# P.V in four groups of four and five steps instead of six groups of three, in the attention of an attention, top-1 MoE and soft MoE kernel on one core

## The chip, the cores and the metric

The kernel runs on one core of one Trainium2 chip. The metric is the device time of one execution in microseconds; lower is better. The engines are called PE (TensorE matmul), PEld (its weight loads), DVE (VectorE), ACT (ScalarE), POOL (GpSimd) and SP (SyncE, which issues DMAs).

## What is computed

Three layers follow each other. Inputs are q, k, v of 4 batches, 8 heads, 1152 positions, 64 wide; the change concerns the first layer alone.

```python
def _attn_ref(q, k, v):
    q_pool = q.reshape(B, H, S // 2, 2, D).mean(axis=3)
    scores = np.matmul(q_pool, k.transpose(0, 1, 3, 2)) / np.sqrt(D)
    scores = scores - np.max(scores, axis=-1, keepdims=True)
    attn = np.exp(scores)
    attn = attn / (np.sum(attn, axis=-1, keepdims=True) + 1e-09)
    return np.matmul(attn, v).astype(np.float32)
...
def reference(...):
    x = attention output, as (B * S / 2, H * D)
    x = _moe_ref(x, ...)    # top-1 of 8 experts: logits, softmax gate, relu FFN of the chosen expert
    return _moe2_ref(x, ...)    # soft MoE with 32 slots
```

## The kernel before

The attention works on 16 pairs of heads, p = 0 to 15 (4 batches of 4 pairs, HP = 4). A pair has 576 pooled queries in two halves u of 288 columns, and 1152 keys in 9 blocks c of 128 (NKB). A **unit** is one (u, c, j): half, key block and head j of the pair. A pair has 36 units, pos = 0 to 35, and a unit has two matmuls into one score buffer of three in PSUM: S1 (line 266, the high part of the product) and S2 (line 272, the low part, with the row maximum subtracted in the same matmul), and then an exponential on ACT (line 276). Two units, j = 0 and 1, make a **step**, 18 to a pair; a step's exponentials lie in one of nine buffers e (EB = 9).

P.V (lines 278 to 289) takes a step's exponentials and two blocks of V, two matmuls per step that the profile shows as four records. It is not done step by step but in **groups** (line 301): three steps at a time (GS = 3), at positions 8, 14, 20, 26, 32 and, for the last three steps of a pair, at position 2 of the next pair (LAG = 3). With each group the steps' exponentials are added up on POOL (accadd, lines 291 to 299), for the softmax sums; in the last pair DVE does most of that. A buffer e comes free when its P.V and its addition have been done.

Between the units, other work of the attention is placed by hand, in a table from position to calls (at, line 569; run at lines 682 and 683, after the unit's S2):

- maxpiece (line 204): a matmul for one of 27 pieces of the row maxima of a later pair, into a PSUM tile of the tag mx (three buffers, shared with nps, sg, sgT, tp and the routing's tiles), and a reduction on DVE (line 219). Positions: MA1, MA, MB, and for pair 0 P0 and P1.
- maxred and maxrow (MR): the maxima of the next pair are gathered on DVE, transposed on PE (nps, line 235) and written into the operand QL on DVE.
- prep (PREP, PREP0) prepares the operands of pair p + 2: two casts kc on ACT (KC), qadd (qs), one cast qc on ACT (QC), two subtractions kl on DVE (KL, line 189), and ql (QLc, line 198), with DMAs on SP that spread each to the tiles KS, KH, QS and QL. qadd and ql run on DVE, in some pairs on POOL.
- fin0, fin1, fin2 (FA for the first half of the queries, FE, FB or FZ for the second, FC): sums and routing logits (sg, lines 319 to 323, and a copy on ACT), their transposes (sgT) with small DVE steps, and the transposes of P.V (tp, line 346) with a product on DVE.
- route (line 352): when a batch's four pairs are done, the routing of its tokens, a queue of small DVE and PE steps, of which line 686 lets one go per permitted position; and 24 **hot** steps per batch, pairs of ACT operations (lines 387 and 388), given out ahead of each group by the table NHOT (line 41, or four a group in the last pairs). A table matmul (tbp) ends it.
- ahead.split: in pairs 14 and 15 a cast on ACT and a subtraction on DVE (lines 796 and 797) for the next layer's first weights, at positions 2, 8, 14, 20, 26 and 32.

The order on every engine is the order in which these calls are made; nothing is reordered. At one position the calls run in this order: S1, S2, the table's work, one constant, one routing step, the hot steps, the group.

Of the kernel before, what the change touches and what calls it, by code (L numbers as in the profile page):

```python
# [87 lines left out]
def attention(ctx, tc, g):  # L88
# [476 lines left out]

    for p in range(n + 1):
        work = {}

        def at(pos, *fs):
            work[pos] = work.get(pos, []) + list(fs)  # L570
# [3 lines left out]
        if p == 0:  # L574
            for i, m in enumerate(range(NP0, NP)):
                at(P0[0] + i * P0[1] // 8, mp(0, m))
            at(P0[0] + P0[1] + 1, lambda: maxred(0, [3, 4]))
# [8 lines left out]
        elif p + 1 < n:
            for pos, m in zip(MA1, range(24)) if p == 1 else zip(MA, range(3, 24)):
                at(pos, mp(p + 1, m))
            if p + 2 < n:
                for pos, m in zip(MB, (24, 25, 26, 0, 1, 2)):  # L590
                    at(pos, mp(p + 2, m))
        if p + 2 < n:
            for pos, f in zip(PREP0 if p == 0 else PREP, prep(p + 2, nc.gpsimd if p == 0 or p >= HP and p % HP < 2 else None)):
                at(pos, f)
        if p < n:
            if p + 1 < n:
                late = 1 if p == 0 else 0
                at(MR[0] + late, lambda: maxred(p + 1, [0, 1, 2, 3, 4]))
                at(MR[1] + late, lambda: maxrow(p + 1))
            late = 4 if p in (0, n - 1) else 2 if p >= HP and p % HP == 0 else 0  # L600
            at(FA[0] + late, lambda: fin0(p, 0))
            at(FA[1] + late, lambda: fin1(p, 0))
# [1225 lines left out]
```

## Time and profile before

| | us |
|---|---|
| runs: median (lowest to highest, 3 runs) | 801.65 (800.77 to 803.76) |
| profiled execution | 804.16 |
| its span, first to last instruction | 802.4 |
| attention, first S1 of pair 0 to last S2 of pair 15 (19.44 to 490.60 of the span) | 471.16 |
| PE busy, of the span | 781.1 |
| DVE, POOL and ACT busy, of the span | 557.7, 470.2 and 463.9 |
| mean granted TensorE clock | 0.998 |

Times are those of one profiled execution, by the hardware profiler. Matmuls are pipelined: their starts are recorded and their ends are modelled, so distances between starts say more than durations. Where a timeline has an idle time in brackets, it is the engine's ahead of that row, with the instruction that ended it. The granted clock is 1 at 2.4 GHz and 0.5 at 1.2 GHz.

### The profile page before, as it was taken

Reading aid. Unit: us, or ns where it says so; the run is one execution under the profiler, and the core shown is the slowest. Engines: PE = TensorE matmul, PEld = TensorE weight load, DVE = VectorE, ACT = ScalarE, POOL = GpSimd, SP = SyncE. Lnnn points to the kernel's source line nnn. Section 1 sums busy time; section 2 is a strip of 40 time slices with the busy share of each in tenths; the row PEclk is TensorE's granted clock in tenths of the full one; section 3 lists DMA queues with packets and bytes.
Section 4 is the critical chain, followed back from the end, with each engine's and each line's share of the span. In section 5 each row is a group of like instructions: output and inputs, shape, how many; then the busy total and the mean of one; then the engine's idle time right before and its main releaser. Section 6 shows DMA issues by size and latency. Waiting matters only on the chain.

```text
span 802.4 us, 16064 instructions
## 1 busy us (share of the span) xinstructions
PE 781.1 (97%) x5696; PEld 598.4 (75%) x5696; DVE 557.7 (70%) x1163; ACT 463.9 (58%) x1101; POOL 470.2 (59%) x429
## 2 busy tenths in 40 slices
PE   5899999999999999999999999999999999999997
PEld 5667777777777777777766667799898789988467
DVE  6867777778777878776878786766666566675242
ACT  5456665665776657776556964355554546554232
POOL 6968899999988987888988964310302211020200
PEclk9999999999999999999999999999999999999999
DMA  9796648675655675664564220677776788976997
GB/s 325 169 270 157 171 138 205 171 217 159 150 157 142 164 210 143 163 169 135 136 151 123 79 81 1 215 236 269 255 286 216 240 293 279 328 256 242 381 394 243
DMA packets 55625, 162.84 MB, mean 203 GB/s; under 512 B 12154, under 2 KB 19626, under 8 KB 51434
## 3 DMA queue, kind: packets, MB, share of 16 engines
q1 hardware_dynamic: 49668, 134.76, 56.0%
q10 hardware_dynamic: 2592, 17.43, 5.9%
q0 software_dynamic: 3280, 9.57, 3.8%
q8 instruction: 47, 0.77, 0.4%
q14 instruction: 38, 0.31, 0.1%
HBM read 110.45 MB, written 10.89 MB: 151 GB/s over the span
## 4 chain that ended last, share of the span: by engine, by line
PE 90%; DVE 6%; ACT 1%; DMA 1%; issue 1%; POOL 0%; ACTq 0%; DVEq 0%
PE pv L286 18%; PE sc L266 12%; PE sc L272 9%; PE mps L217 8%; PE hp L805 4%; PE hp L807 4%; PE hp L806 4%; PE yp L819 4%; PE yp L821 4%; PE yp L820 4%; DVE mxp L219 2%; PE sg L319 2%; PE op L1570 2%; PE hp L1553 2%; PE tp L346 2%; PE tp L784 1%
## 5 line engine op out<-in xcount | busy, mean ns | idle before, releaser
L299 POOL TENSOR_TENSOR acc<-acc,e 128x576 f32<-128x576 f32 x214 | 316.8, 1481 | 20.2 <-ACT e L276 6.7
L276 ACT ACTIVATE e<-sc 128x288 f32<-128x288 f32 x576 | 225.0, 411 | 132.6 <-PE sc L272 113.5
L219 DVE TENSOR_REDUCE mxp<-mps 128x1 f32<-128x384 f32 x432 | 220.5, 549 | 93.9 <-PE mps L217 87.0
L266 PE MATMUL sc<-QS,KS 128*128 128x288 f32 x576 | 185.4, 330 | 1.2 <-ACT e L276 1.0
L272 PE MATMUL sc<-QL,KH 69*128 69x288 f32 x576 | 169.6, 297 | 0.4 <-DVE QL L260 0.3
L286 PE MATMUL pv<-e,V 128*64 128x288 f32 x1152 | 162.1, 417 | 0.0
L266 PEld LDWEIGHTS sc<-QS,KS 128*128 128x128 f32 x576 | 108.8, 189 | 53.1 <-issue 21.2
L217 PE MATMUL mps<-KS,QS 128*128 128x384 f32 x384 | 135.5, 357 | 10.4 <-ACT QS L487 7.1
L286 PEld LDWEIGHTS pv<-e,V 128*64 128x64 f32 x1152 | 74.6, 137 | 61.3 <-issue 23.4
L272 PEld LDWEIGHTS sc<-QL,KH 69*128 69x128 f32 x576 | 108.8, 189 | 0.8 <-POOL QL L490 0.5
L797 DVE TENSOR_TENSOR wlo<-wraw,whi 128x512 fp32r<-128x512 f32 x136 | 90.2, 687 | 23.5 <-ACT whi L796 21.1
L796 ACT CAST whi<-wraw 128x512 fp32r<-128x512 f32 x136 | 79.2, 618 | 11.1 <-DMA wraw<-in_w 5.7
L217 PEld LDWEIGHTS mps<-KS,QS 128*128 128x128 f32 x384 | 74.3, 194 | 15.2 <-ACT QS L487 7.5
L805 PE MATMUL hp<-xh,whi 128*128 128x256 f32 x256 | 73.3, 286 | 0.0
L807 PE MATMUL hp<-xh,wlo 128*128 128x256 f32 x256 | 71.7, 280 | 0.0
L806 PE MATMUL hp<-xl,whi 128*128 128x256 f32 x256 | 71.5, 279 | 0.0
L962 POOL DMA_INDIRECT ls<-both,xidx x17 | 18.0, 1058 | 88.3 <-DVE both L944 45.3
L812 ACT ACTIVATE hh<-hp 128x256 fp32r<-128x256 f32 x64 | 24.6, 384 | 76.4 <-PE hp L807 72.1
L775 POOL DMA_INDIRECT xg<-xs,xidx x17 | 18.8, 1106 | 84.6 <-PE tp L784 51.5
L297 POOL TENSOR_TENSOR acc<-e 128x576 f32<-128x576 f32 x31 | 44.7, 1443 | 35.3 <-ACT e L276 35.2
L813 DVE SCALAR_TENSOR_TENSOR hl<-hp,hh 128x256 fp32r<-128x256 f32 x64 | 27.1, 424 | 44.1 <-ACT hh L812 41.4
L819 PE MATMUL yp<-whi,hh 128*128 128x512 f32 x128 | 52.8, 413 | 0.0
(413 smaller groups left out, 1239.9 us busy)
## 6 DMA issues: line engine op xcount, KB each, us to landing
wraw<-in_w SPq DMA_DIRECT2D x72, 512.0 KB
mw<-in_m2w ACTq DMA_DIRECT2D x16, 1024.0 KB
mw<-in_m2w SPq DMA_DIRECT2D x16, 1024.0 KB
V<-in_vT SPq DMA_DIRECT2D x16, 576.0 KB
KX<-in_kT SPq DMA_DIRECT2D x15, 576.0 KB
QX<-in_qT SPq DMA_DIRECT2D x15, 576.0 KB
KS<-KC SPq DMA_DIRECT2D x30, 288.0 KB
QS<-QC SPq DMA_DIRECT2D x60, 144.0 KB
```

The costliest lines, as they stand in the source:

```text
L217: nc.tensor.matmul(mps[:, :384], s["QS"][:, j, blk * 128:(blk + 1) * 128], s["KS"][:, j, ks], start=True, stop=True)
L219: V.reduce_max(s["mxp"][:, slot, t:t + 1], mps[:, :384], axis=AX.X)
L266: nc.tensor.matmul(sc[:, :NU], s["KS"][:, j, c * 128:(c + 1) * 128], s["QS"][:, j, u * NU:(u + 1) * NU], start=True, stop=False)
L272: nc.tensor.matmul(sc[:, :NU], s["KH"][0:69, j, c * 128:(c + 1) * 128], s["QL"][0:69, j, u * NU:(u + 1) * NU], start=False, stop=True)
L276: nc.scalar.activation(s["e", u, c][:, j], sc[:, :NU], AF.Exp, scale=SM)
L286: nc.tensor.matmul(pv[j * 64:(j + 1) * 64, :NU], s["v"][:, j, c, :], e[:, j], start=(c == 0), stop=(c == NKB - 1))
L299: eng.tensor_add(s["acc", u], s["acc", u], s["e", u, c])
L797: nc.vector.tensor_sub(lo, x, hi.bitcast(F32))
L805: nc.tensor.matmul(hp, wh[:, c], xh[:, k], start=(k == 0), stop=False)
L806: nc.tensor.matmul(hp, wh[:, c], xl[:, k], start=False, stop=False)
L807: nc.tensor.matmul(hp, wl[:, c], xh[:, k], start=False, stop=(k == DM // 128 - 1))
L819: nc.tensor.matmul(yp[h], hh[:, hs], wh, start=(f == 0), stop=False)
```

## The change

The groups end at steps 4, 9, 13 and 18 (ENDS), so they have four, five, four and five steps, and stand at positions 10, 20, 28 and, for the last, 2 of the next pair (GPOS). The buffers stay nine. All the other work is given new positions: the maxima's pieces come in bundles of two or three at places, the preparation, the sums, and the permitted positions of the routing queue (ROOM for pairs 4, 8 and 12 to 15, REST for the others), and the hot steps per group (NHOT 5, 3, 0, 2; HOTL = 6 in pairs 12 to 15). qadd and ql run on POOL in pairs 7, 8, 9, 10 and 12 (PQ), where it was pairs 0, 4, 5, 8, 9, 12 and 13. What is computed, and the number of matmuls, stay the same.

```diff
-NHOT = {2: 2, 8: 0, 14: 2, 20: 2, 26: 2, 32: 4}
+NHOT = {2: 5, 10: 3, 20: 0, 28: 2}
-QSTEP = 2
-GS = 3
+PQ = (7, 8, 9, 10, 12)
+HOTL = 6
+ROOM = {4: (8, 9, 10, 11, 12, 13, 15, 16, 17, 18, 19, 20, 22, 23, 24, 25, 26, 27, 28, 31),
...
+REST = (8, 10, 11, 12, 13, 14, 16, 18, 19, 20, 21, 22, 25, 27, 28, 29, 30, 31, 32, 33, 34, 35)
 LAG = 3
+ENDS = (4, 9, 13, 18)
+GPOS = {2 * e + LAG - 1: i for i, e in enumerate(ENDS[:-1])}
 EB = 9
-P0 = (0, 6)
-P1 = (8, 11, 18)
-LATE = 19
+P0A = (0, 1, 1, 1, 2, 2, 3, 4, 5)
+P0M = (7, 10)
+P1A = (5, 5, 7)
+P1B = (12, 12, 13, 14, 14, 14, 15, 15, 17, 17, 18, 20, 20, 20, 21, 22, 22, 22, 23, 24, 24, 25, 27, 27)
+P2A = (34, 35, 35)
+LATE = 14
-FE = (14, 16, 17)
-PREP = (2, 8, 2, 8, 14, 20, 26)
-PREP0 = (11, 12, 8, 13, 16, 18, 22)
...
-MA = (0, 1, 3, 4, 5, 6, 7, 9, 10, 12, 13, 15, 16, 17, 18, 19, 21, 22, 23, 25, 27)
-MB = (29, 30, 31, 33, 34, 35)
-MR = (29, 32)
-FA = (26, 28, 33)
-FB = (14, 16, 17)
-FZ = (16, 17, 18)
-FC = 7
+FE = (10, 11, 13)
+PREP = (0, 7, 1, 9, 9, 21, 28)
+PREP0 = (11, 12, 11, 20, 18, 20, 29)
...
+MA = (1, 2, 2, 3, 4, 5, 5, 7, 8, 9, 10, 11, 13, 14, 16, 16, 19, 20, 22, 22, 24)
...
+MB = (24, 26, 31, 31, 34, 35)
...
+MR = (25, 28)
+MR2 = (22, 26)
+PREP2 = (3, 10, 0, 10, 10, 18, 20)
...
+FA = (28, 29, 35)
...
+FB = (10, 11, 12)
+FZ = (15, 17, 18)
+FC = 8
@@ group
-        steps = range(GS * g_, GS * g_ + GS)
+        steps = range(ENDS[g_ - 1] if g_ else 0, ENDS[g_])
@@ the loop over pairs: tables chosen by pair
-            for pos, f in zip(PREP0 if p == 0 else PREP, prep(p + 2, nc.gpsimd if p == 0 or p >= HP and p % HP < 2 else None)):
+            for pos, f in zip(PREP0 if p == 0 else PREP if p < n - HP else PREP2, prep(p + 2, nc.gpsimd if p in PQ else None)):
...
@@ the loop over units
-            if queue and pos >= (8 if p < n - 3 else 0) and (pos < MR[0] if p == HP else pos % 3 < 2 if p % HP == 0 or p > n - HP else pos % QSTEP == 0):
+            if queue and pos in ROOM.get(p, REST):
                 queue.pop(0)()
-            if pos % (2 * GS) == LAG - 1 and hot:
-                for f in hots[:4 if p >= n - HP else NHOT[pos]]:
+            if (pos in GPOS or pos == LAG - 1) and hot:
+                for f in hots[:HOTL if p >= n - HP else NHOT[pos]]:
                     hots.pop(0)()
...
             if pos == LAG - 1 and p > 0:
-                group(p - 1, 2 * NKB // GS - 1)
-            elif pos >= 2 * GS and pos % (2 * GS) == LAG - 1:
-                group(p, pos // (2 * GS) - 1)
+                group(p - 1, len(ENDS) - 1)
+            elif pos in GPOS:
+                group(p, GPOS[pos])
```

The change adds 16 lines ahead of maxpiece, so a line of the kernel before stands 16 lower in the kernel after (S1 266 and 282, S2 272 and 288, P.V 286 and 302).

PE, pair 10, the group at position 2 and the units behind it. sc are the scores, mps a piece of the maxima, pv the P.V; x6 are three steps. Before:

```order
L272 MATMUL sc<-QL_149,KH_143 128x288
L286 MATMUL pv<-e,V_162 64x288 x6
L266 MATMUL sc<-QS_146,KS_140 128x288
L272 MATMUL sc<-QL_149,KH_143 128x288
L217 MATMUL mps<-KS_141,QS_147 128x384
```

After:

```order
L288 MATMUL sc<-QL_149,KH_143 128x288
L233 MATMUL mps<-KS_141,QS_147 128x384 x2
L302 MATMUL pv<-e,V_162 64x288 x10
L282 MATMUL sc<-QS_146,KS_140 128x288
L288 MATMUL sc<-QL_149,KH_143 128x288
L233 MATMUL mps<-KS_141,QS_147 128x384
```

The group has five steps where it had three, with two pieces of the maxima directly ahead of it; the next group stands eight units on, where it was six.

DVE, pair 0, from the last writes of pair 0's own maxima (QL) to the gathering of pair 1's (MXZ). mxp is the reduction of a piece, KL one half of kl, qs the operation qadd. Before:

```order
L255 TENSOR_TENSOR QL_148<-nps,mask 5x128
L260 TENSOR_TENSOR QL_148<-nps,mask 5x64
L219 TENSOR_REDUCE mxp<-mps 128x1 x11
L189 TENSOR_TENSOR KL<-KX_151,KC 128x576
L219 TENSOR_REDUCE mxp<-mps 128x1 x3
L189 TENSOR_TENSOR KL<-KX_151,KC 128x576
L219 TENSOR_REDUCE mxp<-mps 128x1 x13
L226 TENSOR_REDUCE MXZ<-mxp 128x2x4
```

After:

```order
L276 TENSOR_TENSOR QL_148<-nps,mask 5x64
L186 TENSOR_TENSOR qs<-QX_153 128x576
L235 TENSOR_REDUCE mxp<-mps 128x1 x11
L205 TENSOR_TENSOR KL<-KX_151,KC 128x576
L235 TENSOR_REDUCE mxp<-mps 128x1 x3
L205 TENSOR_TENSOR KL<-KX_151,KC 128x576
L235 TENSOR_REDUCE mxp<-mps 128x1 x10
L242 TENSOR_REDUCE MXZ<-mxp 128x2x4
```

Among the reductions the two halves of KL keep their places, but they were called at positions 16 and 18, between the groups at 14 and 20, and now at 18 and 20, where the three pieces between them and the second half stand directly ahead of the group of five steps; qs, which POOL did, has come to DVE.

## Rows read from the trace of the kernel before

**Rows 1.** The page: busy time of each engine, and the chain by engine.

```profile
PE 781.1 (97%) x5696; PEld 598.4 (75%) x5696; DVE 557.7 (70%) x1163; ACT 463.9 (58%) x1101; POOL 470.2 (59%) x429
...
PE 90%; DVE 6%; ACT 1%; DMA 1%; issue 1%; POOL 0%; ACTq 0%; DVEq 0%
```

**Rows 2.** Stretches of pairs 0, 10, all: length, busy PE, PEld, DVE, ACT, POOL

```profile
19.44:53.48 34.04, 31.60 (x192) 22.89 (x191) 25.07 (x57) 15.91 (x41) 28.36 (x24) 0.95 0.80 202
...
315.77:344.14 28.37, 28.37 (x198) 20.74 (x198) 21.07 (x45) 22.06 (x56) 23.70 (x17) 1.00 0.60 158
...
sum 471.16, PE 465.06 PEld 335.42 DVE 362.48 ACT 307.31 POOL 410.87; mean PE 29.07 PEld 20.96 DVE 22.65 ACT 19.21 POOL 25.68
```

**Rows 3.** Timeline of PE around a group: start, length, instruction, count

```profile
302.87 0.30 PE L272 MATMUL sc<-QL,KH 69*128 69x288 f32 x1
303.10 1.68 PE L286 MATMUL pv<-e,V 128*64 128x288 f32 x12
304.70 0.40 PE L266 MATMUL sc<-QS,KS 128*128 128x288 f32 x1
304.94 0.29 PE L272 MATMUL sc<-QL,KH 69*128 69x288 f32 x1
...
305.24 0.30 PE L266 MATMUL sc<-QS,KS 128*128 128x288 f32 x1
...
305.69 0.29 PE L266 MATMUL sc<-QS,KS 128*128 128x288 f32 x1
...
306.27 0.30 PE L272 MATMUL sc<-QL,KH 69*128 69x288 f32 x1
...
306.54 0.29 PE L272 MATMUL sc<-QL,KH 69*128 69x288 f32 x1
```

**Rows 4.** Timeline of PE inside that group, in three narrow windows

```profile
303.40 0.65 PE L286 MATMUL pv<-e,V 128*64 128x288 f32 x3
...
303.88 0.65 PE L286 MATMUL pv<-e,V 128*64 128x288 f32 x3
...
304.36 0.41 PE L286 MATMUL pv<-e,V 128*64 128x288 f32 x2
```

**Rows 5.** Stretches behind pair 0's stall; behind POOL stands the granted clock

```profile
36.00:39.40 3.40, 1.93 (x7) 1.24 (x9) 3.40 (x5) 0.73 (x2) 3.32 (x3) 0.81 0.77 191
39.40:42.00 2.60, 2.60 (x13) 1.11 (x10) 2.20 (x4) 0.04 (x1) 0.18 (x1) 0.59 0.53 120
```

**Rows 6.** Timelines of DVE and of PE at pair 0's stall

```profile
35.14 1.81 DVE L189 TENSOR_TENSOR KL<-KX,KC 128x576 fp32r<-128x576 f32 x1
...
37.47 0.44 PE L217 MATMUL mps<-KS,QS 128*128 128x384 f32 x1 [1.60 <-DVE mxp L219]
```

**Rows 7.** Who waited for whom: us in total, times, longest

```profile
PEld tp L346 <- DVE mxp L219: 3.6, 15, 0.3
```

**Rows 8.** Timeline of PE, waits in pairs 13 and 14

```profile
407.95 0.44 PE L217 MATMUL mps<-KS,QS 128*128 128x384 f32 x1 [0.77 <-DVE mxp L219]
...
439.54 0.40 PE L266 MATMUL sc<-QS,KS 128*128 128x288 f32 x1 [0.81 <-ACT e L276]
```

**Rows 9.** Timeline of DVE, five reductions in a row

```profile
319.70 2.42 DVE L219 TENSOR_REDUCE mxp<-mps 128x1 f32<-128x384 f32 x5 [1.01 <-PE mps L217]
```

**Rows 10.** Line 189: count, shortest, median and longest in ns

```profile
L189 DVE TENSOR_TENSOR KL<-KX,KC x28: 740/1243/2000, 35.1 to 420.9; 128x576 fp32r<-128x576 f32 x28
```

**Rows 11.** Timeline of ACT: a cast of KC, exponentials, a cast of weights

```profile
317.78 0.68 ACT L162 CAST KC<-KX 128x576 fp32r<-128x576 f32 x1
...
465.88 1.01 ACT L276 ACTIVATE e<-sc 128x288 f32<-128x288 f32 x3 [0.69 <-PE sc L272]
...
470.54 0.61 ACT L796 CAST KS<-QX 128x512 fp32r<-128x512 f32 x1
```

**Rows 12.** Groups of POOL by line: busy us, mean ns, idle before

```profile
L299 POOL TENSOR_TENSOR acc<-acc,e 128x576 f32<-128x576 f32 x214 | 316.8, 1481 | 20.2 <-ACT e L276 6.7
...
L198 POOL TENSOR_TENSOR QLc<-qs,QC 128x576 fp32r<-128x576 f32 x8 | 11.4, 1420 | 0.1
```

More of the change, by code (lines that the diff above doesn't have):

```diff
@@ L121, in attention @@
     NK2 = NTB // 2
+    UNITS = 4 * NKB
     pieces = [(j, blk, t) for j in range(2) for t in range(3) for blk in range(3)]
@@ L564, in begin @@
         after.extend(later)
+    carry = {}
     for p in range(n + 1):
-        work = {}
+        work, carry = carry, {}
         def at(pos, *fs):
-            work[pos] = work.get(pos, []) + list(fs)
+            w = work if pos < UNITS else carry
+            w[pos % (UNITS)] = w.get(pos % (UNITS), []) + list(fs)
         mp = lambda q, m: (lambda: maxpiece(q, m))
@@ L575, in attention @@
             for i, m in enumerate(range(NP0, NP)):
-                at(P0[0] + i * P0[1] // 8, mp(0, m))
-            at(P0[0] + P0[1] + 1, lambda: maxred(0, [3, 4]))
-            at(P0[0] + P0[1] + 2, lambda: maxrow0(0, [(288, 384), (384, 512), (512, 576)]))
+                at(P0A[i], mp(0, m))
+            at(P0M[0], lambda: maxred(0, [3, 4]))
+            at(P0M[1], lambda: maxrow0(0, [(288, 384), (384, 512), (512, 576)]))
             for i in range(3):
-                at(P1[0] + i, mp(1, 24 + i))
+                at(P1A[i], mp(1, 24 + i))
             for i in range(24):
-                at(P1[1] + i * P1[2] // 24, mp(1, i))
+                at(P1B[i], mp(1, i))
             at(LATE, later)
             for i in range(3):
-                at(33 + i, mp(2, 24 + i))
+                at(P2A[i], mp(2, 24 + i))
         elif p + 1 < n:
-            for pos, m in zip(MA1, range(24)) if p == 1 else zip(MA, range(3, 24)):
+            for pos, m in zip(MA1, range(24)) if p == 1 else zip(MA if p < n - HP else MA2, range(3, 24)):
                 at(pos, mp(p + 1, m))
             if p + 2 < n:
-                for pos, m in zip(MB, (24, 25, 26, 0, 1, 2)):
+                for pos, m in zip(MB if p < n - HP else MB2, (24, 25, 26, 0, 1, 2)):
                     at(pos, mp(p + 2, m))
         if p + 2 < n:
-            for pos, f in zip(PREP0 if p == 0 else PREP, prep(p + 2, nc.gpsimd if p == 0 or p >= HP and p % HP < 2 else None)):
+            for pos, f in zip(PREP0 if p == 0 else PREP if p < n - HP else PREP2, prep(p + 2, nc.gpsimd if p in PQ else None)):
                 at(pos, f)
@@ L596, in attention @@
             if p + 1 < n:
[L597 to L602, printed above, removed]
+                mr = MR0 if p == 0 else MR if p < n - HP else MR2
+                at(mr[0], lambda: maxred(p + 1, [0, 1, 2, 3, 4]))
+                at(mr[1], lambda: maxrow(p + 1))
+            fa = FA0 if p == 0 else FAL if p == n - 1 else FA1 if p >= HP and p % HP == 0 else FA
+            at(fa[0], lambda p=p: fin0(p, 0))
+            at(fa[1], lambda p=p: fin1(p, 0))
             if pairs[p][1]:
-                at(FA[2], lambda: fin2(p, 0))
+                at(fa[2], lambda p=p: fin2(p, 0))
         if p > 0:
@@ L628, in attention @@
         if p == n:
-            group(n - 1, 2 * NKB // GS - 1)
+            group(n - 1, len(ENDS) - 1)
             assert not queue and not hots and not after
```

9 lines of the change are left out of this document (8 added, 1 removed).

## The prediction, on record before the changed kernel ran

> **What bounds the kernel now.** I read the page's shares first. TensorE is busy 781.1 of 802.4 us, and the chain that ended last lies on PE for 90% and on VectorE for 6% [rows 1]. So time is won only where PE's own sequence gets shorter or where PE stops waiting.
>
> Next comes the table of stretches, one head pair of the attention in each [rows 2]. The sixteen pairs take 471.16 us together. An undisturbed one takes 28.37 us (pair 10), with PE busy for all of it, while POOL is busy 23.70, ACT 22.06 and DVE 21.07 us. Pair 0 takes 34.04 us with DVE at 25.07. PE sets the pace, and nobody has more than some 5 us per pair to spare.
>
> The third view is PE's own order of time around one group of P.V [rows 3]. Read the start times, since ends are modelled. A unit (one S1 and one S2) without a piece of the maxima takes 306.54 - 306.27 = 0.27 us, one with a piece 305.69 - 305.24 = 0.45 us. From the S2 ahead of the group (302.87) to the S2 behind it (304.94) are 2.07 us; a unit's 0.27 off leaves 1.80 us for a group of three steps. Inside the group two steps' like records start at 303.40 and 303.88, with three records between them, four records a step [rows 4]: 0.48 us a step, 1.45 us for three (0.243 us for two records, unrounded). So **0.35 us of each group belong to its two ends**, not to its steps: the first record comes 0.23 us after the S2 where half a bare unit, 0.135, is usual; the next pair 0.05 us late; the S1 behind 0.10 us late (304.36 to 304.70), and its S2 again (0.24 for 0.135).
>
> **The change, part by part.** (1) Groups. Six groups of three steps per pair become four of 4, 5, 4 and 5 steps. The steps stay 18 per pair, so the 1152 records stay; 96 groups become 64. 32 x 0.345 = **11.0 us less on PE**, on the path, since PE is busy all through a pair. The sum and weight matmuls (sg) still stand directly ahead of a group in most pairs and share its switch as before; nps alone moves off the group in pairs 13 and 14, at most 2 x 0.345 = 0.7 us, and in pair 0 nps and sg, which stood apart, now share a switch, 0.345 back. I put the rest, 0.35, at nothing.
>
> (2) The stall of pair 0. PE waits 1.60 us for a reduction on DVE, because KL, 1.81 us there [rows 6], stands in the middle of a stretch with nearly a piece per unit. Directly behind it the granted clock has a mean of 0.81 over 3.4 us and 0.59 over 2.6 us [rows 5]: 2 x (0.19 x 3.4 + 0.41 x 2.6) = 3.4 us at the lower level, 1.2 GHz, which lose half, 1.7 us. Together 3.3 us. Afterwards KL's first half stands ahead of the last three pieces and the second directly ahead of the group of five, which covers 5 x 0.485 + 0.345 = 2.8 us. But 14 pieces now lie in the ten units up to this group, and DVE takes 0.465 us for each ((2.42 - 0.56) / 4 [rows 9]), 5.1 us for the eleven ahead of KL against PE's 8 x 0.27 + 11 x 0.175 = 4.1. And behind the group the sixth piece waits for KL's second half. So a wait of about a microsecond stays: I take **2.0 us less**, bounds 0 and 3.3.
>
> (3) Waits elsewhere. The transposes of P.V wait 3.6 us in 15 places for a maxima reduction to free their PSUM buffer [rows 7]; they move to units with few pieces. I take 2.0 us less, bounds 0 and 3.6. Pair 13's piece waits 0.77 us behind routing steps on DVE, and pair 14's S1 0.81 us for exponentials behind hot steps and a cast on ACT [rows 8]. The routing steps get 22 positions in most pairs where they had 14, and the hot steps stand up to five or six together ahead of a group, whose 2.3 to 2.8 us cover them. 1.0 us less, bounds -1.0 (the stretches are denser) and 1.6.
>
> (4) What the change takes cover from. Pairs 14 and 15 hold six casts of the next stage's weights each, 0.61 us on ACT [rows 11], at fixed positions 2, 8, 14, 20, 26 and 32. Each stood ahead of a group; now only 2 and 20 do. A stretch between groups is eight or ten units. Ten exponentials cost ACT 10 x 0.30 = 3.0 us ((1.01 - 0.41) / 2 [rows 11]), against 10 x 0.27 = 2.7 us of PE in pair 15, where there are no pieces; with a cast ACT needs 3.6 us, and three score buffers let PE run three units, 0.8 us, ahead. 8 uncovered casts x 0.61 = 4.9 us at most, 0 at least; near the lower end because of the 0.8 us of slack: **1.0 us more**. KC's casts (0.68 us [rows 11]) stand in the same way ahead of a group or meet 3.0 + 0.7 = 3.7 us of ACT against 2.7 + 7 x 0.175 = 3.9 us of PE: nothing.
>
> (5) The rest. Two more pairs do qadd and ql on DVE and not on POOL (five pairs on POOL, seven before): two operations each, of KL's size and so at most 2.0 us [rows 10], ahead of a group of five and of four, which hide them. The nine exponential buffers: a step's buffer is wanted nine steps, 18 units, later; with the groups at 10, 20, 28 and 38 the shortest distance from the P.V of a step to the next use falls from 10 units to 6 (step 4: group at 20, wanted at 26), still 1.6 us of bare units behind the group: nothing. The last group has five steps and not three after the last unit; the same two steps are missing earlier: nothing. The DMAs of the preparation, on SP's queue, go out a few units earlier or later, with a pair or more until their use: nothing. Everything behind the attention is the same.
>
> Sum against the profiled execution: 804.16 - 11.0 - 2.0 - 2.0 - 1.0 + 1.0 = 789.2 us. It lay 2.5 us above the median of the three runs, 801.65; from the median the same sum gives **786.7 us**, 1.9% less.
>
> The Trainium skill, TensorEngine Tiling (Array Packing), Performance Considerations (Instruction Overhead), gives each matmul about 60 cycles of overhead. By that rule the overhead goes with the matmuls, whose number stays, term (1) is zero and the time is rival (C)'s; the even pace inside a group against the 0.35 us at its ends speaks against it here.
>
> **The rivals.** (A) The forecast, 779 to 793 us: **0.74**.
>
> (B) The ends are saved, but PE waits in the longer stretches for what the groups had covered: DVE's pieces in bundles of two and three at 0.465 us against PE's 0.175, and the casts of (4). It gives back 4.9 us of casts, 1.0 of (3) and 0.7 for nps, and gains nothing in (2): 801.65 - 11.0 + 6.6 = 797.3 us, or less of it. For it: a stretch of ten units has no group in which DVE can catch up. Against it: bundles stand directly ahead of a group. 793 to 797.3: **0.17**.
>
> (C) The group's ends do no harm today because PE would else wait there for exponentials, or the extra goes with the six matmuls of a group, 0.06 us each. Then nothing is gained: 801.65 us. Against it: the two matmuls of a step keep the even pace, and the 0.10 us behind the last record come although score buffers have been free for the whole group. **0.05**.
>
> (D) Slower: POOL becomes the bound. Its 17 additions per pair take 17 x 1.481 = 25.2 us [rows 12], with qadd and ql (1.42 us each) 28.0 us, and the pair shrinks to 28.4 - 0.7 = 27.7. Up to now a pair with both has 0.4 us to spare; from there on POOL falls behind, buffers of exponentials come free late, and the sums wait. At 1.481 the four pairs 7 to 10 lose 0.3 us each, inside the slack of the next half; for a loss the additions must stretch. To undo 11.0 us and 4 more, POOL must need 0.94 us more than PE in each of 16 pairs: that is the point, an addition of (27.7 + 0.94) / 17 = 1.68 us. If each two-operand operation on DVE holds one up by KL's median, 1.24 us [rows 10], POOL needs 25.2 + 4 x 1.24 = 30.2 us in eleven pairs and 28.0 + 2 x 1.24 = 30.5 in the five with preparation: 11 x 2.5 + 5 x 2.8 = 41.5 us more than PE, 801.65 - 11.0 + 41.5 = 832 us. Against it: these operations run beside the additions today, and 214 additions still have a mean of 1.481. **0.04**.
>
> The Trainium skill, SBUF — State Buffer, "two separate sides", says that VectorE with two SBUF inputs and GpSimd lock a shared port, the loser blocking for a whole instruction. The trace bears it out on DVE's side: KL takes from 0.74 to 2.00 us [rows 10].
>
> **How the numbers follow.** About 0.5%, 4 us, is what a measurement of this kernel can tell from no change. Faster needs less than 797.6: A and B, 0.91. Same: C, 0.05. Slower: D, 0.04. The low end: all of (2) and (3), 801.65 - 11.0 - 3.3 - 3.6 - 1.6 = 782, and 3 us of the small waits that no term counts (pair 0 alone is 5.7 us above pair 10, of which (2) counts 3.3): 779. The high end takes in most of B: 796.
>
> **What would show it.** Right: 64 groups, of four steps with 1.94 + 0.35 us and of five with 2.43 + 0.35; an undisturbed pair at 27.5 to 27.8 us; pair 0 at 29 to 32 us; the sixteen pairs at about 456 us; no lower clock, or a shorter one, near 40 us. B: waits of S1 for exponentials or of pieces for reductions, in sum over 5 us. D: POOL busy all through pairs 7 to 10, and sg or exponentials waiting for the additions. Wrong in its root: groups whose ends cost more than 0.35 us, or a pair still at 28.4.

## The result, and the profile after

The changed kernel takes **794.25 us** (median of 5 runs, 793.52 to 796.22) against 801.65 (median of 5 runs on the same chip, 800.77 to 804.97): ratio 0.990, 95% interval 0.988 to 0.993. It is faster by 7.4 us, 0.9%. The forecast was 786.7, so the direction came as forecast, and half of the gain.

Of the two profiled executions the one of before (804.16 us) lay 2.5 us above its median, that of the change (793.52) 0.7 below its own. So the traces differ by 10.6 us of span where the medians differ by 7.4, and the tally below is made against the 10.6.

The page of the changed kernel, busy time and the chain by engine and by line (compare [rows 1]):

```profile
PE 767.4 (97%) x5696; PEld 598.8 (76%) x5696; DVE 556.4 (70%) x1167; ACT 448.4 (57%) x1101; POOL 470.7 (59%) x425
...
PE 83%; DVE 7%; DMA 5%; ACT 2%; issue 1%; POOL 1%; SPq 1%; ACTq 0%; DVEq 0%; POOLq 0%
PE pv L302 15%; PE sc L282 10%; PE sc L288 8%; PE mps L233 7%; PE hp L823 4%; PE hp L825 4%; PE hp L824 4%; PE yp L837 4%; PE yp L839 4%; PE yp L838 4%; DVE mxp L235 3%; DMA KH<-KC 2%; PE sg L335 2%; PE op L1588 2%; PE hp L1571 2%; PE tp L362 1%
```

PE's busy time fell by 13.7 us with the same 5696 matmuls, but its share of the chain fell too, from 90% to 83%: DVE (6% to 7%) and DMA (1% to 5%) end more of the waits. A DMA, KH<-KC, is new among the lines. Lines of the changed kernel are 16 higher than those of the kernel before from the attention on.

The stretches of pairs 0 and 10 and the sum over the sixteen pairs (compare [rows 2]; length, then busy PE, PEld, DVE, ACT, POOL, granted clock, DMA share, GB/s):

```profile
19.80:49.92 30.12, 29.55 (x185) 21.76 (x183) 25.44 (x62) 15.96 (x42) 26.02 (x21) 1.00 0.80 207
...
309.07:336.50 27.43, 27.43 (x200) 20.70 (x198) 18.71 (x43) 19.93 (x54) 24.67 (x18) 1.00 0.62 164
...
sum 458.88, PE 450.02 PEld 334.89 DVE 358.56 ACT 291.28 POOL 409.08; mean PE 28.13 PEld 20.93 DVE 22.41 ACT 18.20 POOL 25.57
```

The sixteen pairs lost 12.28 us; the span before them grew by 0.36 and the one behind them by 1.32, of which 0.97 are the two more steps of the last group. Pair 10 went from 28.37 to 27.43 us, a little below the range named.

A group of five steps in pair 10 of the changed kernel, in the timeline of PE (compare [rows 3]):

```profile
324.08 0.34 PE L233 MATMUL mps<-KS,QS 128*128 128x384 f32 x1
324.35 2.65 PE L302 MATMUL pv<-e,V 128*64 128x288 f32 x20
326.92 0.40 PE L282 MATMUL sc<-QS,KS 128*128 128x288 f32 x1
327.16 0.30 PE L288 MATMUL sc<-QL,KH 69*128 69x288 f32 x1
```

From the piece to the S2 behind the group are 3.08 us; without a group, a piece and an S1 take 0.17 + 0.135 there. 2.78 us are left, and five steps of 0.485 and one pair of ends of 0.345 make 2.77. So the ends cost the longer group what they cost the shorter one.

Read pair by pair, the loss shows. This table has the length of a pair (from its first S1 to that of the next) in the kernel before, the changed one, and the main experiments. The last row counts **spells**: unbroken stretches on PE of P.V, sg, sgT, nps or tp (and of cps, a small count that the routing of pair 13 makes), which matmuls of S1, S2, the maxima or the rest of the routing end; one of them, a nps, stands ahead of pair 0. Each has two ends, as a group has.

| pair | before | changed | threes | groups alone | calm | queue edits | both edits |
|---|---|---|---|---|---|---|---|
| 0 | 34.05 | 30.12 | 33.52 | 31.00 | 30.09 | 30.13 | 30.24 |
| 1 | 30.14 | 30.69 | 30.77 | 31.44 | 30.85 | 28.95 | 28.99 |
| 2 | 28.39 | 27.47 | 28.83 | 29.25 | 27.50 | 27.48 | 27.46 |
| 5 | 30.48 | 30.53 | 33.79 | 30.27 | 28.97 | 30.51 | 29.28 |
| 6 | 28.59 | 27.43 | 29.16 | 29.54 | 28.59 | 27.45 | 28.27 |
| 8 | 29.30 | 29.28 | 30.17 | 31.77 | 27.96 | 28.02 | 27.92 |
| 9 | 29.61 | 31.59 | 31.95 | 32.27 | 34.38 | 30.75 | 33.35 |
| 10 | 28.37 | 27.43 | 29.34 | 29.55 | 27.96 | 27.45 | 28.47 |
| 13 | 32.28 | 32.12 | 34.15 | 33.24 | 32.15 | 32.13 | 32.12 |
| 14 | 30.51 | 28.11 | 35.86 | 31.45 | 28.11 | 28.14 | 28.13 |
| 15 | 26.11 | 26.33 | 24.90 | 25.80 | 26.35 | 26.35 | 26.37 |
| all 16 | 471.15 | 458.88 | 487.85 | 485.02 | 460.63 | 455.13 | 458.33 |
| spells | 169 | 138 | 186 | 160 | 138 | 138 | 138 |

Pairs 2, 6 and 10, undisturbed and without routing, fell by 0.9 us or more, pairs 0 and 14 by more than two. Pairs 1, 5, 8 and 9, which hold routing steps or follow pair 0's preparation, fell by nothing or grew.

A part of this is work that changed its pair. The routing's table, six matmuls tbp, stands in pairs 7, 11 and 14 before and in pairs 8, 12 and 15 now. The timelines of PE, before in pair 7 and after in pair 8:

```profile
246.07 0.87 PE L381 MATMUL tbp<-rR,rA 96*72 96x256 f32 x6
246.77 0.29 PE L266 MATMUL sc<-QS,KS 128*128 128x288 f32 x1
...
255.08 0.87 PE L397 MATMUL tbp<-rR,rA 96*72 96x256 f32 x6
255.78 0.30 PE L282 MATMUL sc<-QS,KS 128*128 128x288 f32 x1
```

From the first start to that of the S1 behind are 0.70 us in both. So 0.7 us of the fall of pair 14 is this move, and pairs 8 and 15 had to make up for as much. These six show no ends either: they take 0.12 us each, and S1 comes 0.12 us behind the last start. The kernel declares their operands as fp32r, like those of S1 and S2, and those of P.V as f32; that the change of type makes the ends would fit, but no run varied it.

The waits of PE are of two kinds. The first, in pair 5 of the changed kernel, in the timeline of PE:

```profile
179.84 0.44 PE L233 MATMUL mps<-KS,QS 128*128 128x384 f32 x1 [0.18 <-DVE mxp L235]
...
185.40 0.45 PE L230 MATMUL mps<-KC,QB 128*128 128x384 f32 x1 [0.73 <-DVE mxp L235]
```

What DVE did in that time, in its timeline:

```profile
178.10 1.23 DVE L425 CAST rdi<-dest 96x6 int32<-96x6 f32 x1
...
181.38 0.92 DVE L428 CAST rdf<-rdi 96x12 f32<-96x12 int32 x1
...
182.83 1.97 DVE L205 TENSOR_TENSOR KL<-KX,KC 128x576 fp32r<-128x576 f32 x1
```

The piece waits for a reduction, and DVE is busy with a cast of 96x6 that takes 1.23 us and a KL of 1.97. The second kind, in pairs 1 and 9, is DMAs. The timeline of ACT in pair 1:

```profile
55.20 0.67 ACT L178 CAST KC<-KX 128x576 fp32r<-128x576 f32 x1 [4.07 <-DMA KH<-KC]
```

The timeline of SP, which issues the transfers, at the end of pair 0 and in pair 9:

```profile
48.45 2.00 SPq L171 DMA_DIRECT2D KH<-KC  x2
...
289.29 7.54 SPq L171 DMA_DIRECT2D QS<-QC  x4
297.16 1.51 SPq L171 DMA_DIRECT2D QB<-QC  x2
```

The timeline of PE at the two waits:

```profile
56.23 0.40 PE L282 MATMUL sc<-QS,KS 128*128 128x288 f32 x1 [1.27 <-ACT e L292]
...
301.18 0.41 PE L230 MATMUL mps<-KC,QB 128*128 128x384 f32 x1 [0.63 <-DMA QB<-QC]
```

The cast to KC, at the head of ACT's order in pair 1, waits 4.07 us until a DMA of the last preparation has read KC; the exponentials stand behind it, and S1 waits for those. In pair 9 the DMA engines are full (share 1.01 to 1.06 from 283 to 292 us), SP needs 7.54 us to issue four transfers, and QB, last in line, lands late.

### The profile page after: what moved, and what is told of

The parts are those of the page before. It is cut to its first block, busy times and chain, and to the rows that moved or that the text cites. A ratio compares the mean times of both kernels' runs of the same rounds, so it can differ in the third digit from the quotient of the medians.

```text
span 791.8 us, 16027 instructions
## 1 busy us (share of the span) xinstructions
PE 767.4 (97%) x5696; PEld 598.8 (76%) x5696; DVE 556.4 (70%) x1167; ACT 448.4 (57%) x1101; POOL 470.7 (59%) x425
## 4 chain that ended last, share of the span: by engine, by line
PE 83%; DVE 7%; DMA 5%; ACT 2%; issue 1%; POOL 1%; SPq 1%; ACTq 0%; DVEq 0%; POOLq 0%
PE pv L302 15%; PE sc L282 10%; PE sc L288 8%; PE mps L233 7%; PE hp L823 4%; PE hp L825 4%; PE hp L824 4%; PE yp L837 4%; PE yp L839 4%; PE yp L838 4%; DVE mxp L235 3%; DMA KH<-KC 2%; PE sg L335 2%; PE op L1588 2%; PE hp L1571 2%; PE tp L362 1%
## 5 line engine op out<-in xcount | busy, mean ns | idle before, releaser
L315 POOL TENSOR_TENSOR acc<-acc,e 128x576 f32<-128x576 f32 x214 | 322.4, 1507 | 22.3 <-ACT e L292 7.7
L292 ACT ACTIVATE e<-sc 128x288 f32<-128x288 f32 x576 | 216.0, 412 | 103.8 <-PE sc L288 92.5
L235 DVE TENSOR_REDUCE mxp<-mps 128x1 f32<-128x384 f32 x432 | 218.2, 550 | 72.2 <-PE mps L233 63.3
L282 PE MATMUL sc<-QS,KS 128*128 128x288 f32 x576 | 178.4, 326 | 1.3 <-ACT e L292 1.3
L288 PE MATMUL sc<-QL,KH 69*128 69x288 f32 x576 | 164.5, 297 | 0.3 <-DVE QL L276 0.3
L302 PE MATMUL pv<-e,V 128*64 128x288 f32 x1152 | 153.8, 412 | 0.0
L233 PE MATMUL mps<-KS,QS 128*128 128x384 f32 x384 | 126.5, 357 | 11.7 <-ACT QS L503 7.4
L302 PEld LDWEIGHTS pv<-e,V 128*64 128x64 f32 x1152 | 77.0, 136 | 63.1 <-issue 18.8
L233 PEld LDWEIGHTS mps<-KS,QS 128*128 128x128 f32 x384 | 71.8, 193 | 18.3 <-DVE mxp L235 8.0
```

What stands on the lines that cost most here:

```text
L233: nc.tensor.matmul(mps[:, :384], s["QS"][:, j, blk * 128:(blk + 1) * 128], s["KS"][:, j, ks], start=True, stop=True)
L235: V.reduce_max(s["mxp"][:, slot, t:t + 1], mps[:, :384], axis=AX.X)
L282: nc.tensor.matmul(sc[:, :NU], s["KS"][:, j, c * 128:(c + 1) * 128], s["QS"][:, j, u * NU:(u + 1) * NU], start=True, stop=False)
L288: nc.tensor.matmul(sc[:, :NU], s["KH"][0:69, j, c * 128:(c + 1) * 128], s["QL"][0:69, j, u * NU:(u + 1) * NU], start=False, stop=True)
L292: nc.scalar.activation(s["e", u, c][:, j], sc[:, :NU], AF.Exp, scale=SM)
L302: nc.tensor.matmul(pv[j * 64:(j + 1) * 64, :NU], s["v"][:, j, c, :], e[:, j], start=(c == 0), stop=(c == NKB - 1))
```

## The experiments

**Threes: the groups undone.**

```diff
-ENDS = (4, 9, 13, 18)
+ENDS = (3, 6, 9, 12, 15, 18)
-NHOT = {2: 5, 10: 3, 20: 0, 28: 2}
+NHOT = {2: 5, 8: 3, 14: 0, 20: 0, 26: 2, 32: 0}
```

> The changed kernel with six groups of three steps again (all other positions as changed). Theory, the ends of a group cost 0.345 us each: 32 more groups, 11.0 us more, so about 805 us, and an undisturbed pair (3, 6, 10) goes from 27.4 us to 28.1. Rival, the gain came from the new positions of pieces, preparation and sums: within 2 us of the changed kernel's 794.25, undisturbed pairs still at 27.4. If groups of three also bring back waits that the new positions do not fit, the time lies above 805 and the pairs' waits show it.

821.49 us (4 runs, 820.94 to 823.41), ratio to before 1.022 (1.018 to 1.027). That is above both expectations, the case that the last sentence left open. The stretch of pair 2:

```profile
83.95:112.78 28.83, 28.79 (x200) 20.47 (x198) 21.53 (x46) 16.55 (x44) 25.41 (x29) 1.00 0.59 157
```

Pair 2 goes from 8 spells to 12, not 10: nps and sg, placed directly ahead of a group of the changed kernel, now stand by themselves. 28.83 - 27.47 = 1.36 us for four spells is 0.34 us each. Pairs 3, 6 and 10, which the expectation named, also have four spells more and rose by 1.63, 1.73 and 1.91 us; PE is idle for 0.06, 0.28 and 0.45 us in them (not at all in the changed kernel), and without that it is 0.36 to 0.39 us per spell. So the price of a group's ends is borne out, about, and nps and sg pay it too where they stand alone; for sgT and tp by themselves it was not measured. In the sum 48 more spells make 48 x 0.345 = 16.6 of 28.97 us. Of the rest, 5.1 us are idle time of PE (13.9 us in the sixteen pairs, 8.9 in the changed kernel), the largest part in pair 14. In pairs 5, 13 and 14 the mean granted clock is 0.95, where it was 1.00: by an estimate from their 104 us, some 5 us more.

**Groups alone, with everything else at its old place.**

```diff
-GS = 3
+ENDS = (4, 9, 13, 18)
+GPOS = {2 * e + LAG - 1: i for i, e in enumerate(ENDS[:-1])}
-NHOT = {2: 2, 8: 0, 14: 2, 20: 2, 26: 2, 32: 4}
+NHOT = {2: 2, 10: 2, 20: 4, 28: 4}
...
-                for f in hots[:4 if p >= n - HP else NHOT[pos]]:
+                for f in hots[:6 if p >= n - HP else NHOT[pos]]:
```

> The kernel before with its P.V groups changed to 4, 5, 4 and 5 steps and the hot steps moved with them; maxima, preparation, sums and routing stay at their old positions. Theory, ends at 0.345 us each on an always busy PE: 801.65 - 11.0 = 790.7 us, undisturbed pairs 28.37 - 0.69 = 27.7. Rival, the new positions are needed because the longer stretches otherwise let PE wait for reductions and exponentials: 5 us or more come back in waits, 796 us or more, and the undisturbed pairs stand above 27.9.

821.84 us (819.93 to 825.53), ratio 1.023 (1.018 to 1.028): the rival, by more than it said. Only 9 spells are saved, since sg and nps lost their group, and the waits grow: PE is idle for 22.2 us of the sixteen pairs, where it was 6.1. From the table of waits of this kernel (who waits for whom, us in total, times, longest):

```profile
PE mps L218 <- DVE QL L241: 12.2, 13, 2.0
```

One of them in the timeline of PE, in pair 10:

```profile
352.19 0.41 PE L218 MATMUL mps<-KS,QS 128*128 128x384 f32 x1 [0.81 <-DVE QL L241]
```

The maxima's transpose nps at position 32 had a group at its side; without one, the piece behind it waits for QL's rows on DVE. The groups alone lose 2.3%, the new positions with the old groups 2.2%; together they gain 1.0%.

**Pair 1: what holds KH<-KC up.** Two edits, one each.

```diff
-LATE = 14
+LATE = 19
```

> The changed kernel with the late loads of pair 0 at position 19, where they stood, and not at 14. In the changed kernel S1 of pair 1 waits 1.4 us because the cast to KC waits 4.07 us for the DMA KH<-KC, which is issued 7 us later after the start of the pair than before. Theory L, the 2.3 MB of loads that now go out ahead of the preparation's DMAs hold those up: the wait goes, pair 1 falls from 30.7 to about 29.3 us. Theory Q, the cast to QC moved from position 13 to 20 holds up the DMAs behind it in order: pair 1 stays at 30.7 within 0.3 us.

```diff
-PREP0 = (11, 12, 11, 20, 18, 20, 29)
+PREP0 = (11, 12, 11, 13, 18, 20, 29)
```

> The changed kernel with pair 0's cast to QC at position 13, where it stood, and not at 20. Theory Q (the cast's place holds up the DMAs that follow it in SP's queue): KH<-KC goes out some 3 us or more earlier, the wait of 1.4 us goes, pair 1 falls to about 29.3 us. Theory L (the late loads ahead of them): pair 1 stays at 30.7 within 0.3 us.

794.71 us and 799.66 us, one run each. With the loads at 19 pair 1 takes 30.87 us; this tells nothing against theory L, since the cast to QC stands at 20, and on SP's queue the loads still go out ahead of it. With the cast at 13 pair 1 takes 34.83 us: a piece waits 3.12 us for KS<-KL, which stands behind the loads as before, and the mean granted clock of the pair is 0.90. So theory Q, which expected 29.3, fell, and what stands behind the loads waits.

**The loads behind the preparation, and the casts of pairs 14 and 15 ahead of groups.**

```diff
-LATE = 14
+LATE = 21
...
-                at(6 * i + 2, lambda i=i: ahead.split(i))
+                at((2, 10, 10, 20, 20, 28)[i], lambda i=i: ahead.split(i))
```

(and the same for the six casts of pair 15.)

> The changed kernel with two edits in pairs that do not touch each other. (a) Pair 0's late loads at position 21, behind the second half of KL, so that on SP's queue the preparation's DMAs (QB, QS, KS, KH) go out ahead of the loads; with the loads at 19 they had gone out in the same order as in the changed kernel, so that run could not tell. Theory L (the loads hold up KH<-KC): KH goes out near 42 us instead of 48.5, S1's wait of 1.4 us in pair 1 goes, pair 1 takes 29.2 to 29.5 us instead of 30.7. Rival: the cast to KC waits for another DMA in its place and pair 1 stays above 30.3. (b) The twelve casts of the next stage's weights in pairs 14 and 15 directly ahead of groups (positions 2, 10, 10, 20, 20 and 28). Theory of my term (4), uncovered casts cost about 1.0 us over both pairs: pairs 14 and 15 together fall from 54.4 to about 53.4. Rival, the slack of three score buffers hides them: 54.4 within 0.3.

797.70 us, one run. (a) Pair 1 falls to 29.15 us: theory L. But pair 0 takes 32.86. 0.92 us of its growth are a wait for exponentials 13.9 us into the pair, which the run with the cast at 13 has too, without this edit. Another 1.13 us are a wait for wgbd, a small weight that sg needs and that went back with the loads, as its timeline of PE shows:

```profile
48.60 0.66 PE L339 MATMUL sg<-xu,wgbd 128*16 128x288 f32 x2 [1.13 <-DMA wgbd<-in_wg]
```

(b) Pair 15 stays (26.30 us for 26.33), so ACT's casts were covered there. Pair 14 takes 32.35 us for 28.11. The casts' second halves on DVE, now two together in a row of its timeline, hold the reductions up, a piece waits 1.75 us, and the mean granted clock of the pair is 0.95:

```profile
433.50 2.15 DVE L815 TENSOR_TENSOR KS<-KX,KS 128x512 fp32r<-128x512 f32 x1
435.58 1.90 DVE L815 TENSOR_TENSOR KH<-QX,KH 128x512 fp32r<-128x512 f32 x1
```

Neither theory had that.

**Without POOL's additions in three pairs.**

```diff
-        elif c > 1:
+        elif c > 1 and p not in (5, 9, 13):
```

> The changed kernel without POOL's running additions in pairs 5, 9 and 13, but for the first of each half (the sums of the exponentials of these pairs are left out, and with them the right scale of their rows). Theory P: PE waits in these pairs because the routing's small steps on VectorE and KL are held until an addition on POOL ends (a cast of 96x6 took 1.23 us there and 0.16 us elsewhere): these steps now take 0.15 to 0.25 us, KL 0.75, the waits of PE for reductions go, and pairs 5, 9 and 13 fall from 30.5, 31.6 and 32.1 us by about 1.2, 2.0 and 2.3 us. Rival N: it is the number of steps and pieces in the stretch, or DMAs that come late: the pairs stay within 0.5 us and the steps keep their length.

The total (905.73 us) is not comparable, since the tables of later stages come from those sums; only pairs are read. Pair 5 falls from 30.53 to 29.02 us, and the rows that answer to the three above are, in the timeline of DVE:

```profile
177.16 0.16 DVE L425 CAST rdi<-dest 96x6 int32<-96x6 f32 x1
...
178.97 0.16 DVE L428 CAST rdf<-rdi 96x12 f32<-96x12 int32 x1
...
179.66 0.74 DVE L205 TENSOR_TENSOR KL<-KX,KC 128x576 fp32r<-128x576 f32 x1
```

1.23 and 0.92 us have become 0.16, KL's 1.97 has become 0.74, and both waits of the pair are gone: theory P for pair 5. Pair 13 falls by 1.2 us, half of what was expected: one of its two waits stays, behind a step of 96x48 that still took 1.30 us, from 396.70 on, beside the first addition, which this kernel keeps (396.53, 1.41 us). Reductions of the same small sizes take 0.17 to 0.22 us with and without additions. Pair 9 rises to 34.20: its waits on DVE are gone too, but its piece waits longer for QB (1.92 us), and the mean granted clock of the pair is 0.90. So pair 9 has a second cause, the DMAs, and there theory N holds.

**Calm: fewer positions for routing.**

```diff
-REST = (8, 10, 11, 12, 13, 14, 16, 18, 19, 20, 21, 22, 25, 27, 28, 29, 30, 31, 32, 33, 34, 35)
+REST = (10, 20, 25, 27, 28, 29, 30, 32, 33)
-8: (8, 10, 12, 13, 15, 16, 18, 20, 21, 22, 23, 25, 27, 30, 31, 32, 33, 34)
+8: (8, 10, 18, 20, 25, 27, 28, 29, 30, 31, 32, 33, 34)
```

> The changed kernel with fewer positions for routing steps: 9 in most pairs in place of 22, all directly ahead of a group or behind position 24, where hardly any piece of the maxima stands, and in pair 8 eight in place of twelve from position 18 on. Theory R (the dense positions put routing steps among the bundled pieces, and PE waits for the reductions behind them): pair 5 falls from 30.5 to about 29.3 us, pair 8 from 29.3 to 28.3, pair 9 from 31.6 to about 29.8, pair 6 and 10 rise by less than 0.5. Rival K: the second half of KL behind the group at 20, or the DMAs, make these waits: pairs 5, 8 and 9 fall by less than 0.5 us each.

795.24 us, one run. Pairs 5 and 8 fall as theory R has it, to 28.97 and 27.96 us; for pair 8 that is weak, since two kernels with no edit there took 28.0 as well, where five took 29.2 to 29.3. But the steps that leave pair 5 turn up in pair 6 (28.59, up 1.16), and pair 10 pays 0.53. Pair 9 takes 34.38 us: its piece waits 1.96 us for QB, and its mean granted clock is 0.95. In sum nothing is won.

**SP's queue put in order.** wgbd at 14, the large loads at 21; QB ahead of QS.

```diff
             at(LATE, later)
+            at(21, loads)
...
-            if p <= 2:
-                qb()
+            qb()
             for j in range(2):
                 d(s["QS"][0:64, j], QC[j * 64:(j + 1) * 64])
                 d(s["QS"][64:128, j], QC[j * 64:(j + 1) * 64])
-            if p > 2:
-                qb()
```

> The changed kernel with two edits of SP's queue. (a) Pair 0: only the small weight of the gate (wgbd) is loaded at position 14; the large loads of V, KX and QX go out at 21, behind the preparation's DMAs. With all of them at 21 pair 1 fell by 1.5 us, but sg of pair 0 waited 1.5 us for wgbd. Theory L: both waits are gone, pairs 0 and 1 together fall from 60.8 us to about 59.3. Rival: the loads come too late for the next preparation, and pair 1 or 2 waits for KX. (b) QB goes out ahead of QS in every preparation. Theory D (in pair 9 the DMAs are full behind the write of xr, and QB, last of its preparation, holds a piece up): the wait of 0.80 us at 23.7 us of pair 9 goes, pair 9 falls from 31.6 to about 30.8 us, pairs 5, 6, 10 stay. Rival: another reason on VectorE, pair 9 stays within 0.3 us.

790.85 us, one run. Pairs 0 and 1 take 60.04 us together (60.81 in the changed kernel; pair 0 started 1.1 us earlier here and waited 0.94 us for exponentials 13.9 us into it). Pair 9 takes 30.87. The same kernel with more runs, "queue edits":

> The kernel with the two edits of SP's queue alone, timed: the waits of pairs 1 and 9 that it removed are 1.7 and 0.7 us, so it lies some 2 to 3 us below the changed kernel's 794.25 us, near 791.5, and below 0.99 of the kernel before.

**791.16 us** (6 runs, 790.22 to 796.27), ratio to before 0.986 (0.983 to 0.988), where the changed kernel's was 0.990. Pairs 0 and 1 take 59.08 us. The intervals of the two touch, but the waits are gone in both profiles. The two profiles of this one kernel also show how much a pair can differ between executions: pair 0 took 31.09 and 30.13 us, pair 8 29.25 and 28.02. In the profile of the timed run, the stretches of pairs 1 and 9:

```profile
49.88:78.83 28.95, 28.93 (x205) 21.59 (x204) 22.75 (x50) 16.61 (x44) 24.24 (x29) 1.00 0.86 239
274.45:305.20 30.75, 29.64 (x209) 21.89 (x209) 23.65 (x56) 17.44 (x47) 27.55 (x19) 1.00 0.84 222
```

And SP's timeline at the end of pair 0 and in pair 9:

```profile
41.84 1.90 SPq L171 DMA_DIRECT2D KH<-KC  x2
...
286.07 2.46 SPq L171 DMA_DIRECT2D QB<-QC  x2
```

KH<-KC goes out 6.6 us earlier than in the changed kernel; QB goes out 11.6 us into pair 9, where it was 19.7. Both theories L and D hold.

**Routing steps elsewhere, on top of this.** REST with 11 and with 9 positions; pair 8 without 21 to 24, but for 23 in the second.

```diff
-REST = (8, 10, 11, 12, 13, 14, 16, 18, 19, 20, 21, 22, 25, 27, 28, 29, 30, 31, 32, 33, 34, 35)
+REST = (8, 10, 11, 12, 13, 14, 16, 25, 27, 28, 30)
```

> The kernel with the two edits of SP's queue, and routing steps moved: from 22 positions to 11 in most pairs (8, 10 to 14, 16, and 25, 27, 28, 30), none between 18 and 24, where pieces stand two and three together with the second half of KL, and in pair 8 none between 21 and 24. Theory R: pair 5 falls from 30.5 to about 29.3 us (the wait at 22.6 us goes, a part of that at 17 stays), pair 8 to 28.3, pair 9 to about 29.5, pairs 6 and 10 stay within 0.3. Rival: the steps' length on VectorE follows POOL's additions wherever they stand, so the waits only move, and the sum of pairs 5 to 10 stays within 1 us of the kernel without this edit.

```diff
-REST = (8, 10, 11, 12, 13, 14, 16, 18, 19, 20, 21, 22, 25, 27, 28, 29, 30, 31, 32, 33, 34, 35)
+REST = (10, 13, 20, 25, 27, 28, 29, 30, 31)
```

> As the run before, with 9 positions (10, 13, 20, 25 and 27 to 31) instead of 11: directly ahead of groups and behind position 24 but for one. Theory R: pair 5 near 29.0 as with the nine calm positions, and because nothing stands behind 31, VectorE's backlog at the start of pairs 6 and 9 (waits of 1.0 and 0.8 us there) is smaller: pair 6 near 27.9, pair 9 near 29.7. Rival: the backlog comes from the number of steps behind 24, and pair 6 stays near 28.6.

806.29 and 805.87 us, one run each. Both edits left pair 8 too few positions: the write of xr slid behind pair 9's load on SP's queue, and the next xr waited for it on DVE, so that pair 9 took 46.3 and 46.9 us. The timeline of PE in the first of the two:

```profile
294.66 0.69 PE L332 MATMUL sg<-acc,ones 128*32 128x288 f32 x2 [12.14 <-DVE xr L360]
```

And of DVE:

```profile
293.96 0.55 DVE L360 TENSOR_TENSOR xr<-tp,rs 96x384 f32<-96x384 f32 x1 [11.98 <-DMA xs<-xr]
```

Of the rest, pair 5 takes 30.14 with 11 positions and 29.29 with 9, pair 6 27.44 and 28.22. So with 9 positions pair 5 gives 1.2 us and pair 6 takes 0.8 of it, as the rival has it; with 11 pair 5 gives 0.4, a third of what theory R expected, and pair 6 takes nothing.

**Both edits: nine positions, with the write of xr in its place.** REST is that of the second of the two runs before; pair 8 gets more positions.

```diff
+8: (8, 10, 18, 19, 20, 25, 27, 28, 29, 30, 31, 32, 33)
```

> The two edits of SP's queue, and the nine calm positions for routing with eleven positions from 18 on in pair 8, so that the write of xr keeps its place in SP's queue ahead of the load of pair 9 (in the two runs before it slid behind that load, and pair 9 waited 12 us for it). Theory R with theory D: pair 5 and 6 together 57.5 us (58.0 with the queue's edits alone), pair 8 28.0 (29.3), pair 9 30.2 or less (30.9), pair 10 up to 28.0 (27.4); in sum about 2 us less than the queue's edits alone, near 789 us. Rival: pair 9 waits in another place and the sum does not fall.

791.38 us (790.46 to 793.28), ratio 0.985 (0.983 to 0.987): no better than the queue's edits alone. Pairs 5 and 6 take 57.55 us, pair 8 27.92, as expected; but pair 9 takes 33.35, since a piece still waits for QB, though QB goes out at 285.77 us, as early in the pair as with the queue's edits alone, and behind that wait the clock falls. The DMA engines, behind the write of xr and three loads, have a share of 1.01 and 0.94 from 285 to 291 us, but 0.35 in the next 3 us; what held QB for so long is not shown. The timeline of PE, and then the stretch behind:

```profile
296.58 0.41 PE L227 MATMUL mps<-KC,QB 128*128 128x384 f32 x1 [1.17 <-DMA QB<-QC]
```

The stretch (granted clock behind POOL):

```profile
298.00:301.00 3.00, 3.00 (x15) 2.21 (x15) 1.41 (x4) 1.23 (x3) 3.00 (x3) 0.50 0.91 227
```

Half of full speed is the lower level, 1.2 GHz: 1.5 of these 3 us are lost. Against the queue's edits alone theory R gains 1.2 us in pair 5, and pair 8 took 28.02 without it too; pairs 6 and 10 give back 0.8 and 1.0 us, pair 9 2.6.

## Why the prediction was half right

Against the profile the forecast was -15.0 us; the traces differ by -10.6. Where a pair's change is split, its spells are taken at 0.345 us.

**(1) Groups, -11.0: right.** 31 spells fewer are 10.7 us. The price per end held for groups of five and, in the threes, as a dose (0.34 us per spell in pair 2). That nps and sg share a group's ends was named as a detail; it is more than half of the matter, since the groups alone saved 9 spells of the 31. Rival (C) fell, and with it what the Trainium skill's TensorEngine Tiling (Array Packing), Performance Considerations, would give by its overhead per matmul: the number of matmuls stayed at 5696.

**(2) Pair 0, -2.0: right.** It fell by 3.93 us: 1.04 for three spells, 0.97 for two steps that moved into the next pair, and 1.9 for the stall. The granted clock is 1.00 now all through it, where [rows 5] had 0.81 and 0.59; KL took 1.19 and 0.74 us where [rows 6] had 1.81.

**(3) Waits elsewhere, -2.0 and -1.0: the first right, the second is where the prediction failed.** The transposes' waits of [rows 7] are gone from the table of waits, and pairs 2, 3, 4, 6, 7, 10 and 11 fell by 3.4 us beyond their spells; 1.4 of that is the table's matmuls, which left pairs 7 and 11, so 2.0 us are waits. Pair 14 fell by 2.05 beyond its own, 0.7 of it for the same reason, pair 13 kept its time. But the step "routing steps get 22 positions ... 1.0 us less, bounds -1.0 and 1.6" allowed a loss of 1.0 us and took the denser stretches for harmless: pairs 5 and 9 lost 1.08 + 2.67 = 3.75 us beyond their spells, some 0.8 of it for a DMA (see (5)). A routing step was counted by its size; on DVE it lasts, unless it is a reduction, until an addition on POOL is through. The rows of before had this for KL [rows 10], and it was used only there; its trace had it for the cast too (count, shortest, median and longest in ns):

```profile
L409 DVE CAST rdi<-dest x4: 156/474/1182, 185.8 to 502.6; 96x6 int32<-96x6 f32 x4
```

Leaving the additions out showed it in pair 5, and in pair 9 for its waits on DVE. The Trainium skill, SBUF — State Buffer, two separate sides, has the loser of the shared port block for a whole instruction, and counts among VectorE's operations those of a fast two-port mode beside those with two SBUF inputs. The trace agrees: the cast of 96x6 took 1.23 us beside additions and 0.16 without; that this cast, with its one input, runs in that mode is not shown. Pair 8 lost 0.67 us beyond its spells, which is the 0.7 us of the table's matmuls that came into it; its own two waits, 1.0 us in sum, came and went between executions of one kernel.

**(4) Casts without cover, +1.0: not borne out.** In pair 15 they cost nothing that could be moved away. Pair 15 rose by 0.9 us against its spells, and pair 12 by 0.4, but the table's 0.7 us came into both, in pair 15 with a wait of 0.54 us behind its fifth matmul. The prediction had no term for this move; in the sum it is nothing.

**(5) The rest, nothing: wrong for SP's DMAs.** "With a pair or more until their use" overlooked that KC is one buffer: the next cast to it waits until the DMAs have read it, and that is early in the next pair. The late loads had slid ahead of them in the queue. And QB of pair 9 is wanted in the pair in which it goes out: issued 19.7 us into it, waited for at 23.7. 1.24 us in pair 1 and about 0.8 of the 2.67 in pair 9 are this; the queue's edits won back 1.7 and 0.8. The remark on the two steps of the last group was right: 0.97 us stand behind the attention and are missing in pair 0.

The tally: -10.7 for spells, -0.97 for the steps that moved and -1.9 in pair 0, -2.0 in undisturbed pairs, -1.35, -0.34 and -0.16 in pairs 14, 12 and 13, then 1.24 + 1.08 + 2.67 + 0.2 back in pairs 1, 5, 9 and 15, and the table's matmuls out of three pairs and into three: within 0.1 of -12.28. With 0.36 ahead of and 1.32 behind the attention, -10.6. The 3.2 us to the medians' -7.4 are the position of the two profiled executions.

So the time is in **rival (B)**'s band, 793 to 797.3, and its sign came, some 7 us of waits; but it was a weak sign, since PE is idle for 8.9 us of the sixteen pairs now and was for 6.1 before. Its mechanism, bundles of pieces and uncovered casts, did not: undisturbed pairs have no such wait, and ACT's casts were covered. **(D)** did not come: POOL's additions went from a mean of 1481 to 1507 ns, and POOL is busy 24.67 of pair 10's 27.43 us. They slow DVE, not themselves.

What stays open is a place for the routing steps that wins in pairs 5 and 9 and does not give it back in 6, 9 and 10, and the waits of pair 13. The queue's edits, alone or with the nine positions, are the best versions measured: clearly below the kernel before, and by their ratios to it (0.986 and 0.985) below the changed kernel's 0.990, with intervals that touch for the first and not for the second.

## What to carry to other kernels

Count not only the groups but every stretch on PE that has such ends, and place the small ones at the side of a large one; first see in the trace which have them, since the table's six matmuls had none. Then move the groups and the positions together, since either alone lost over 2% here. A small step on DVE beside a busy POOL is to be priced by POOL's instruction, not by its own size. When a step with DMAs is moved, write down the order on the queue, and ask who waits to overwrite what they read.

## What the runs showed that was not expected

A cast of 6 elements a partition took from 0.16 to 1.23 us, by what POOL did. A wait of PE of 1.17 us in pair 9 of the kernel with both edits was followed by a granted clock of 0.50 over 3 us, while one of 1.27 us in pair 1 of the changed kernel left it at 1.00. And a transfer of 16 KB, early in its queue (issued from 285.8 us), still kept PE waiting at 296.6, though the DMA engines, full to 291 us behind the 1170 KB of xr and the loads, had a share of only 0.35 from 291 to 294.
